# The shift's rounded part straight from ScalarE, its full value and difference on GpSimd, in an attention kernel on one core

## The chip, the cores and the metric

The program runs on one core of a Trainium2 chip. The metric is the device time of one execution in microseconds. A core has five engines with queues of their own: TensorE (PE, with its weight loads shown apart as PEld), VectorE (DVE), ScalarE (ACT), GpSimd (POOL) and SyncE (SP), which here issues nearly all DMAs. Each works through its queue in the order in which the program was built, and waits at an instruction until what that needs is ready.

## The reference

One block of a transformer with adaptive layer norm, on 2048 rows of 512, with 32 heads of 16:

```python
def _A_ref(x, wqkv, wo):
    ...
    scores = jnp.einsum("bhqd,bhkd->bhqk", q, k) * (Dh ** -0.5)
    p = _softmax(scores, axis=-1)
    o = jnp.einsum("bhqk,bhkd->bhqd", p, v)
    return (lambda x, *d: x.transpose(*d))(o, 0, 2, 1, 3).reshape(B, S, D) @ wo
...
mod = (_silu(c) @ w_mod).reshape(c.shape[0], 6, 1, -1)
sa, ca, ga, sb, cb, gb = (mod[:, 0], mod[:, 1], mod[:, 2], mod[:, 3], mod[:, 4], mod[:, 5])
h = _layernorm(x, axis=-1) * (1 + ca) + sa
x = x + ga * _A_ref(h, A_wqkv, A_wo)
h = _layernorm(x, axis=-1) * (1 + cb) + sb
x = x + gb * _B_ref(h, B_w1, B_w2, B_w3, B_w4)
```

`_B_ref` is a mixer: layer norm, `w1` and gelu, shifts along the rows, `w2`, then layer norm, `w3` and gelu, `w4`, with residuals. The change is inside the softmax of `_A_ref`.

## The kernel before

**Precision.** Matrices are used as a rounded upper part (type `F32R`) and the difference to it, so a product takes three matmuls (`mm3`, lines 359, 361 and 363 of its lines in the profile, for `k`, `q`, `v` and the mixer's `w`).

**Units.** Attention goes through 64 units: four chunks of 512 queries, and in each 16 pairs of heads. A unit has 16 steps, one for each 128 keys, and each step has two halves, one for each head `j` of the pair. A step does the following.

- *Maxima.* `max_part` (lines 996 and 992) works 24 steps ahead: PE computes scores with queries on the partitions into a bank `mb`, VectorE takes their row maximum into `mx`. One reduction of 128x512 for each half step.
- *Shift.* When the last maximum of a unit is there, `max_fin` (lines 1042 to 1045) makes the unit's shift, 26 ln 2 minus the maximum, for each of the 8 x 128 queries: VectorE's small reduction `mf`, the full value in place on ScalarE, its rounded upper part `nm[:, 0]` on ScalarE, the difference `nm[:, 1]` on GpSimd. Eight small DMAs (`shift_rows`) write both parts as two more rows of the queries' tile `qtl`, whose partners in the keys' tile `kst` are rows of ones: the matmul itself adds the shift.
- *Scores and exponentials.* `score_part` (lines 1012 and 1008): PE computes the shifted scores with keys on the partitions into a bank `sc`, ScalarE writes their exponential as 32-bit whole numbers into `pt`.
- *Halving.* `p_low` (line 1061 on GpSimd, or line 156 on ScalarE) turns the low 16 bits of 128x1024 of these into half-precision numbers. The planner picks the engine that it thinks is free first.
- *Output.* `pv_part`: PE multiplies the upper words (line 1086) and, two blocks later, the halved low words (line 1083) by `v` into one bank `pv`. At a unit's end ScalarE copies it to `ac` (line 1103), PE transposes it (`ot`, line 1113), and ScalarE (line 1120), VectorE and GpSimd (line 1124) divide by the sums into `osb`.

Seven banks are shared by `mb`, `sc` and the other work's results. Each is free again when VectorE or ScalarE has read it.

**What sets the order.** The program is written by a planner, `Sched`: it keeps a supposed time for each engine (`T`) and puts instructions into the queues as those times advance. A chain like the one of the shift is a list of (engine, supposed ns, function); `misc` puts its parts between the exponentials (ACT), maxima (DVE) and halvings (POOL) where they fit. The supposed costs so decide where everything else goes, and which engine gets a halving:

```python
g, a = [max(sch.T[e], ready) for e in "GA"]
if g > a + LACT:
```

**Stages.** The layer norm, the modulation and the first projections come first. Units 0 to 12 have the rest of the projections `v`, `k` and `q` between their steps, as the planner's fill (with ScalarE's `qk` roundings, line 353, and weight pieces, lines 881 to 896). Units 13 to 61 are attention alone. After that come the output projection and the mixer (`tail`), which begin within units 62 and 63.

Of the kernel before, what the change touches and what calls it, by code (L numbers as in the profile page):

```python
# [14 lines left out]
AF = mybir.ActivationFunctionType  # L15
OP = mybir.AluOpType
# [16 lines left out]
PEXP = PBITS * 0.6931471805599453  # L33
# [297 lines left out]
def kernel(ctx, tc, A_x, A_wqkv, A_wo, B_w1, B_w2, B_w3, B_w4, c, w_mod, out):  # L331
    nc = tc.nc
    te, act, dve, pool, dma = nc.tensor, nc.scalar, nc.vector, nc.gpsimd, nc.sync
# [21 lines left out]
    def mark(key):  # L355
        return None, 0, lambda: done.add(key)
# [623 lines left out]
    def max_part(m, j):  # L980

        u, i = divmod(m, 16)
        c, g = divmod(i, 4)
        if u not in mxs:
            mxs[u] = at.tile([P, 2, 4, NC], F32, name="mx", tag="mx", bufs=2)
        x, b = bank("mb")
        ready, sm.t[x] = sm.t[x], LATE
        r = slice(64 * j, 64 * j + 62)
        lhs = qst[u][r, (g // 2) * 256:(g // 2 + 1) * 256].rearrange("p (n l) -> p l n", l=2)[:, g % 2]

        def after(e):
            end = sch.crit("D", 605, e + PX, lambda: dve.reduce_max(mxs[u][:, j, g, c:c + 1], b, axis=AX.X))  # L992
            sm.t[x] = end + XP["D"]
            if (c, g, j) == (NC - 1, 3, 0):
                max_fin(u)
        return ready, lambda: te.matmul(b, lhs, kst[u % 3][r, c * CH:(c + 1) * CH], start=True, stop=True), after  # L996
# [32 lines left out]
    def max_fin(u):  # L1029
        mf = at.tile([P, 8], F32, name="mf", tag="mf", bufs=2)  # L1030
        nm = at.tile([P, 2, 8], F32R, name="nm", tag="nm", bufs=2)
        mx = mxs.pop(u)

        def shift_rows():
            for j in range(2):
                for i in range(2):
                    r = 64 * j + 62 + i
                    for h in range(2):
                        sch.dma(dma.dma_start,
                                qst[u][r:r + 1, h * 256:(h + 1) * 256].bitcast(F32).rearrange("o (p l) -> o p l", l=2),  # L1040
                                nm[:, i, 4 * j + 2 * h:4 * j + 2 * h + 2].bitcast(F32))
        sch.chain(("D", 85, lambda: dve.reduce_max(mf.rearrange("p (j g) -> p j g", j=2), mx, axis=AX.X)),
                  ("A", 100, lambda: act.activation(mf, mf, AF.Copy, scale=-1.0, bias=PEXP)),
                  ("A", 100, lambda: act.activation(nm[:, 0], mf, AF.Copy)),
                  ("G", 250, lambda: pool.tensor_tensor(nm[:, 1], mf, nm[:, 0], op=OP.subtract)),
                  (None, 0, shift_rows), mark(("shift", u)), prio=0, ready=sch.T["D"])

    def p_low(s):
# [553 lines left out]
    for k, blk in enumerate(blocks + [[]] * (LAG + CPER)):  # L1602
# [35 lines left out]
        low = sorted(e_exp)  # L1638
# [92 lines left out]
```

## Time and profile before

| | |
|---|---|
| runs | 2022.35, 2021.24, 2019.19 us; median 2021.24 |
| profiled execution | 2021.44 us, of which the span from first to last instruction is 2019.7 us |
| granted TensorE clock over the span | 0.992 |
| shifts | 64, one for each unit, first at 121 us, last at 1492 us |
| line 1043 / 1044 (ScalarE) | 64 each, median 220 / 209 ns |
| line 1045 (GpSimd) | 64, median 203 ns |
| shift DMAs `qtl<-nm` | 512, 1.0 KB each, median 2.0 us to landing |
| halvings | 953 on GpSimd, mean 1367 ns; 71 on ScalarE |

In rows of groups stand line, engine, operation, what is written and read, shapes and count, then busy us and mean ns of one, then the engine's idle time just before them and what ended it. In rows of a stretch stand its ends, its length, busy time (and count) of PE, PEld, DVE, ACT and POOL, then the granted clock, the DMA engines' busy share and GB/s. In rows of the chain, the work that ended last followed backwards, stand start, length and name. In rows of the timeline a run of equal instructions is one row, with its start, its length from first start to last end, and the count behind the x.

### The profile page before, as it was taken

The numbers are of one execution on the slowest core, as the hardware profiler recorded it, in microseconds if no ns is written. First come the engines' busy times: TensorE is split into PE (matmuls) and PEld (weight loads), VectorE is DVE, ScalarE is ACT, GpSimd is POOL, SyncE is SP. The second block draws the span as 40 slices with busy tenths as digits, with TensorE's granted clock in tenths as the row PEclk, the third lists the DMA queues.
The fourth block names the chain that finished last, engine by engine and source line by source line (L and its number), as shares of the span: only waits on it lengthen the run. The fifth ranks groups of instructions, "written<-read, shape, count | busy, mean of one in ns | idle before, by whom it ended". The sixth has DMA issues, their size and how long they took to land.

```text
span 2019.7 us, 41655 instructions
## 1 busy us (share of the span) xinstructions
PE 1934.4 (96%) x14456; PEld 1162.1 (58%) x14456; DVE 1656.3 (82%) x2979; ACT 1510.2 (75%) x3085; POOL 1571.9 (78%) x1488
## 2 busy tenths in 40 slices
PE   7999999999999999999999999999998999999999
PEld 5755545454444444444444444444455878898998
DVE  6398888879999999999999999999975886556443
ACT  6438987768999999999999999999985544344443
POOL 6349988879999999999999999999996554435222
PEclk9989999999999999999999999999999999999999
DMA  8777675445343434444443435354414676553541
GB/s 295 233 204 192 151 187 155 135 130 124 86 92 87 91 88 83 96 82 97 81 98 75 104 72 107 72 136 126 99 46 158 230 261 265 226 200 116 201 153 68
DMA packets 185508, 278.01 MB, mean 138 GB/s; under 512 B 117104, under 2 KB 127856, under 8 KB 169008
## 3 DMA queue, kind: packets, MB, share of 16 engines
q1 hardware_dynamic: 181792, 267.20, 49.1%
q10 hardware_dynamic: 2304, 4.20, 0.6%
q0 software_dynamic: 1200, 3.93, 0.5%
q8 instruction: 115, 1.88, 0.4%
q14 instruction: 97, 0.79, 0.1%
HBM read 211.81 MB, written 62.91 MB: 136 GB/s over the span
## 4 chain that ended last, share of the span: by engine, by line
PE 61%; DVE 16%; ACT 9%; issue 6%; POOL 4%; DMA 3%; SPq 0%; ACTq 0%; POOLq 0%; DVEq 0%
PE mb L996 13%; DVE mx L992 12%; PE pv L1086 9%; PE sc L1012 8%; ACT pt L1008 7%; PE w L363 5%; PE w L359 5%; PE w L361 5%; PE pv L1083 4%; PE ot L1113 3%; POOL pt L1061 2%; PE xT L1247 1%; POOL trs L1356 1%; PE v L359 1%; DMA wr<-Ws 1%
## 5 line engine op out<-in xcount | busy, mean ns | idle before, releaser
L1061 POOL TENSOR_SCALAR pt<-pt 128x1024 f16<-128x1024 uint16 x953 | 1248.3, 1367 | 79.9 <-ACT pt L1008 76.7
L992 DVE TENSOR_REDUCE mx<-mb 128x1 f32<-128x512 f32 x2048 | 1250.0, 681 | 72.7 <-PE mb L996 63.5
L1008 ACT ACTIVATE pt<-sc 128x512 int32<-128x512 f32 x2048 | 1060.9, 614 | 123.5 <-PE mb L996 97.1
L996 PE MATMUL mb<-kst,qtl 62*128 62x512 f32 x2048 | 781.1, 461 | 20.5 <-ACT pt L1008 10.0
L1012 PE MATMUL sc<-qtl,kst 64*128 64x512 f32 x2048 | 739.3, 449 | 4.6 <-DVE mx L992 1.8
L996 PEld LDWEIGHTS mb<-kst,qtl 62*128 62x128 f32 x2048 | 358.9, 193 | 233.7 <-ACT pt L1008 160.4
L1012 PEld LDWEIGHTS sc<-qtl,kst 64*128 64x128 f32 x2048 | 336.6, 185 | 185.4 <-DVE mx L992 118.7
L1086 PE MATMUL pv<-pt,vst 128*32 128x512 f16 x4096 | 384.8, 397 | 20.6 <-ACT ac L1103 20.6
L1460 POOL TENSOR_TENSOR g<-sq,g 128x256 fp32r<-128x256 f32 (+1 forms) x124 | 96.8, 785 | 188.9 <-ACT g L1459 176.6
L1083 PE MATMUL pv<-pt,vst 128*32 128x512 f16 (+1 forms) x2048 | 220.8, 389 | 2.5 <-POOL pt L1061 2.4
L1086 PEld LDWEIGHTS <-vst 128*32 128x32 bf16 x4096 | 91.8, 93 | 227.2 <-issue 208.8
L361 PE MATMUL w<-A,wr 128*128 128x256 f32 (+1 forms) x520 | 153.4, 295 | 0.3 <-DVE A L349 0.3
L359 PE MATMUL w<-A,wr 128*128 128x256 f32 (+1 forms) x520 | 153.2, 295 | 0.3 <-ACT A L353 0.3
L363 PE MATMUL w<-A,wr 128*128 128x256 f32 (+1 forms) x520 | 153.1, 294 | 0.0
L1456 ACT ACTIVATE sq<-w 128x256 f32<-128x256 f32 (+1 forms) x130 | 52.1, 401 | 127.0 <-PE w L363 117.5
L363 PE MATMUL w<-wr,g 128*128 128x512 f32 x270 | 106.5, 394 | 3.1 <-POOL g L1460 3.1
L359 PE MATMUL w<-wr,g 128*128 128x512 f32 x270 | 106.9, 396 | 1.8 <-DMA wr<-Ws 1.8
L361 PE MATMUL w<-wr,g 128*128 128x512 f32 x270 | 106.1, 393 | 0.0
L1438 DVE SCALAR_TENSOR_TENSOR sq<-sq,w 128x256 f32<-128x256 f32 (+1 forms) x130 | 58.1, 449 | 56.5 <-ACT sq L1458 56.3
L359 PEld LDWEIGHTS w<-A,wr 128*128 128x128 f32 x520 | 98.7, 190 | 1.7 <-ACT A L353 0.5
L361 PEld LDWEIGHTS w<-A,wr 128*128 128x128 f32 x520 | 98.7, 190 | 1.6 <-DVE A L349 0.5
L363 PEld LDWEIGHTS w<-A,wr 128*128 128x128 f32 x520 | 98.6, 190 | 0.5 <-issue 0.5
(156 smaller groups left out, 2131.6 us busy)
## 6 DMA issues: line engine op xcount, KB each, us to landing
wr<-Ws SPq DMA_DIRECT2D x66, 1024.0 KB, 5.2
vst<-Vs SPq DMA_DIRECT2D x64, 768.0 KB, 5.7
kst<-Ks SPq DMA_DIRECT2D x126, 384.0 KB, 6.1
Ws<-wr SPq DMA_DIRECT2D x14, 1024.0 KB, 5.0
qtl<-Qs SPq DMA_DIRECT2D x128, 96.0 KB, 4.3
Vs<-vt SPq DMA_DIRECT2D x32, 384.0 KB, 4.2
Ks<-qk SPq DMA_DIRECT2D x16, 512.0 KB, 3.8
Qs<-qk SPq DMA_DIRECT2D x16, 512.0 KB, 3.0
```

The source lines that it names most:

```text
L359: te.matmul(o, lh, rh, start=first, stop=False)
L361: te.matmul(o, lh, rl, start=False, stop=False)
L363: te.matmul(o, ll, rh, start=False, stop=last)
L992: end = sch.crit("D", 605, e + PX, lambda: dve.reduce_max(mxs[u][:, j, g, c:c + 1], b, axis=AX.X))
L996: return ready, lambda: te.matmul(b, lhs, kst[u % 3][r, c * CH:(c + 1) * CH], start=True, stop=True), after
L1008: ea = sch.crit("A", 480, e + PX, lambda: act.activation(pt[s][:, j], b, AF.Exp))
L1012: return ready, lambda: te.matmul(b, kst[u % 3][r, kt * P:(kt + 1) * P], qst[u][r], start=True, stop=True), after
L1061: e_low[s] = XP["G"] + sch.crit("G", 1345, ready, lambda: pool.tensor_scalar(o, i, 0.5, 1.0, op0=OP.mult, op1=OP.mult))
L1083: te.matmul(acc[r:r + n, :], v[:, kt + i, c:c + n].bitcast(F16), pt[s + i].bitcast(F16)[:, j, 0::2], start=False, stop=kt == NKT - 2, skip ...
L1086: te.matmul(acc[r:r + 32, :], v[:, kt, r:r + 32], pt[s].bitcast(F16)[:, j, 1::2], start=kt == 0, stop=False, skip_group_check=True)
L1113: te.matmul(b[:, t * n:(t + 1) * n], ac[:, t * P:(t + 1) * P], smat.rearrange("p j d -> p (j d)"), start=True, stop=True)
L1460: ("G", cG(n), lambda: pool.tensor_tensor(lo, sq, hi, op=OP.subtract)), (None, 0, end), bank=b)
```

## The change

ScalarE no longer makes the full value. It computes the shift from the maxima and rounds it in one instruction (new line 1047). GpSimd makes the full value in place from the maxima and then the difference (new lines 1035 and 1036). The planner's list has one ScalarE entry of 100 ns fewer, and GpSimd's is 450 in place of 250.

```diff
@@ max_fin
         mx = mxs.pop(u)
 
+        def low():
+            pool.tensor_scalar(mf, mf, -1.0, PEXP, op0=OP.mult, op1=OP.add)
+            pool.tensor_tensor(nm[:, 1], mf, nm[:, 0], op=OP.subtract)
+
         def shift_rows():
...
         sch.chain(("D", 85, lambda: dve.reduce_max(mf.rearrange("p (j g) -> p j g", j=2), mx, axis=AX.X)),
-                  ("A", 100, lambda: act.activation(mf, mf, AF.Copy, scale=-1.0, bias=PEXP)),
-                  ("A", 100, lambda: act.activation(nm[:, 0], mf, AF.Copy)),
-                  ("G", 250, lambda: pool.tensor_tensor(nm[:, 1], mf, nm[:, 0], op=OP.subtract)),
+                  ("A", 100, lambda: act.activation(nm[:, 0], mf, AF.Copy, scale=-1.0, bias=PEXP)),
+                  ("G", 450, low),
                   (None, 0, shift_rows), mark(("shift", u)), prio=0, ready=sch.T["D"])
```

The order of the queues changes with it. Lines from 1034 on have numbers that are 3 or 4 higher: 1047 stands for 1043 and 1044, 1035 and 1036 for 1045, 1064 for 1061, 1106 for 1103, 1123 for 1120 and 1127 for 1124; line 156 keeps its number.

First, GpSimd around the shifts of units 27 and 28, in attention alone (`pt` are halvings, `osb` is a finished unit's division). Before:

```order
L1045 TENSOR_TENSOR nm<-mf,nm 128x8
L1061 TENSOR_SCALAR pt<-pt 128x1024 x15
L1045 TENSOR_TENSOR nm<-mf,nm 128x8
L1124 TENSOR_TENSOR osb_7627<-sm,rc 128x4x32
L1061 TENSOR_SCALAR pt<-pt 128x1024 x11
```

Now:

```order
L1036 TENSOR_TENSOR nm<-mf,nm 128x8
L1064 TENSOR_SCALAR pt<-pt 128x1024 x15
L1035 TENSOR_SCALAR mf<-mf 128x8
L1036 TENSOR_TENSOR nm<-mf,nm 128x8
L1127 TENSOR_TENSOR osb_7627<-sm,rc 128x4x32
L1064 TENSOR_SCALAR pt<-pt 128x1024 x11
```

One instruction more stands at the same place; the halvings around it are unmoved.

Second, ScalarE in units 30 and 31, from the copy `ac` in the one to that in the other (`pt<-sc` are exponentials, `pt<-pt` on line 156 is a halving). Before:

```order
L1008 ACTIVATE pt<-sc 128x512 x15
L1103 ACTIVATE ac<-pv 128x512
L1008 ACTIVATE pt<-sc 128x512 x3
L1120 ACTIVATE sm<-ot 128x136
L1008 ACTIVATE pt<-sc 128x512 x6
L156 ACTIVATE pt<-pt 128x1024
L1008 ACTIVATE pt<-sc 128x512 x3
L1043 ACTIVATE mf<-mf 128x8
L1044 ACTIVATE nm<-mf 128x8
L1008 ACTIVATE pt<-sc 128x512 x21
L156 ACTIVATE pt<-pt 128x1024
L1103 ACTIVATE ac<-pv 128x512
```

Now:

```order
L156 ACTIVATE pt<-pt 128x1024
L1008 ACTIVATE pt<-sc 128x512 x3
L1106 ACTIVATE ac<-pv 128x512
L1008 ACTIVATE pt<-sc 128x512 x3
L1123 ACTIVATE sm<-ot 128x136
L1008 ACTIVATE pt<-sc 128x512 x12
L1047 ACTIVATE nm<-mf 128x8
L1008 ACTIVATE pt<-sc 128x512 x6
L156 ACTIVATE pt<-pt 128x1024
L1008 ACTIVATE pt<-sc 128x512 x12
L1106 ACTIVATE ac<-pv 128x512
```

The halving that stood right ahead of unit 31's copy has gone from there, and one has come three exponentials ahead of unit 30's. The same happens in units 42 and 43 and in 54 and 55; in unit 13 the halving ahead of the copy goes too. In the other units between 16 and 61 ScalarE's row is unmoved but for the missing line 1043, or moved by a few places.

Third, ScalarE in units 11 and 12, from one shift to the next, where the last projections are (`qk<-q` is the rounding behind 12 fill matmuls of `q`). Before:

```order
L1044 ACTIVATE nm<-mf 128x8
L1008 ACTIVATE pt<-sc 128x512 x12
L353 ACTIVATE qk_163<-q 128x512
L1008 ACTIVATE pt<-sc 128x512 x9
L1103 ACTIVATE ac<-pv 128x512
L1008 ACTIVATE pt<-sc 128x512 x6
L353 ACTIVATE qk_165<-q 128x512
L1120 ACTIVATE sm<-ot 128x136
L1008 ACTIVATE pt<-sc 128x512 x9
L1043 ACTIVATE mf<-mf 128x8
```

Now:

```order
L1047 ACTIVATE nm<-mf 128x8
L1008 ACTIVATE pt<-sc 128x512 x12
L353 ACTIVATE qk_165<-q 128x512
L1008 ACTIVATE pt<-sc 128x512 x9
L1106 ACTIVATE ac<-pv 128x512
L1008 ACTIVATE pt<-sc 128x512 x3
L1123 ACTIVATE sm<-ot 128x136
L1008 ACTIVATE pt<-sc 128x512 x12
L1047 ACTIVATE nm<-mf 128x8
```

The last rounding of `q` now stands one unit's copy earlier: the projections end in unit 11.

## The prediction

> **What bounds the kernel now.** I read the first part of the page, then a table of the stages by stretch, then groups, waits and chain of the long middle stretch, and last one of its units instruction by instruction.
>
> ```profile
> span 2019.7 us, 41655 instructions
> PE 1934.4 (96%) x14456; PEld 1162.1 (58%) x14456; DVE 1656.3 (82%) x2979; ACT 1510.2 (75%) x3085; POOL 1571.9 (78%) x1488
> ```
>
> PE is the fullest engine, but its busy time counts overlapping, modelled matmuls; the shares also average over stages. The stretches show more (length, then busy time of PE, weight loads, VectorE, ScalarE, GpSimd):
>
> ```profile
> 0.00:131.10 131.10, 116.61 (x544) 82.33 (x544) 80.41 (x167) 59.57 (x118) 54.53 (x73) 0.97 0.78 240
> 131.10:477.10 346.00, 335.88 (x2553) 180.63 (x2554) 287.59 (x490) 271.81 (x563) 303.04 (x259) 0.98 0.63 164
> 477.10:1468.50 991.40, 959.17 (x8168) 454.76 (x8170) 950.47 (x1654) 916.69 (x1814) 951.04 (x811) 1.00 0.44 94
> 1468.50:1535.00 66.50, 63.69 (x490) 33.55 (x490) 42.28 (x78) 50.83 (x104) 61.11 (x61) 1.00 0.20 61
> 1535.00:2019.70 484.70, 459.08 (x2712) 410.86 (x2710) 295.55 (x594) 211.32 (x488) 202.18 (x287) 0.99 0.52 191
> ```
>
> Units 0 to 12 fill the second row, with projections mixed in; the third is attention alone, half of the span, where PE, VectorE and GpSimd are all busy 96 to 97% and ScalarE 92%. The change puts work on and off two engines of a balanced loop. From 550.9 to 1468.5 us, 45 units, the groups (count, busy us, mean ns, idle before) and waits (total, times, longest) are:
>
> ```profile
> L992 DVE TENSOR_REDUCE mx<-mb 128x1 f32<-128x512 f32 x1441 | 876.0, 681 | 31.1 <-PE mb L996 24.9 <-PE sc L1012 3.1
> L1061 POOL TENSOR_SCALAR pt<-pt 128x1024 f16<-128x1024 uint16 x661 | 860.5, 1363 | 31.9 <-ACT pt L1008 29.4
> L156 ACT ACTIVATE pt<-pt 128x1024 f16<-128x1024 uint16 x60 | 82.5, 1375 | 0.0
> L1043 ACT ACTIVATE mf<-mf 128x8 f32<-128x8 f32 x45 | 10.7, 237 | 0.0
> L1044 ACT ACTIVATE nm<-mf 128x8 fp32r<-128x8 f32 x45 | 9.4, 209 | 1.6 <-ACT mf L1043 0.2
> L1045 POOL TENSOR_TENSOR nm<-mf,nm 128x8 fp32r<-128x8 f32 x45 | 9.1, 203 | 2.4 <-ACT nm L1044 2.0
> ```
> ```profile
> PEld mb L996 <- ACT pt L1008: 132.8, 390, 0.8
> PE pv L1086 <- ACT ac L1103: 17.5, 15, 1.2
> ```
>
> VectorE idles 31 us in 918, so its maxima are the floor. PE waits most for ScalarE's exponentials to free banks. One stall is regular: 15 times in 45 units PE stands 1.17 us until ScalarE has copied the finished output (`ac`).
>
> The chain of that stretch gives the removed instruction a share:
>
> ```profile
> by line: PE mb L996 20.9%; DVE mx L992 18.8%; PE pv L1086 14.4%; PE sc L1012 12.6%; ACT pt L1008 12.5%; issue 7.6%; PE pv L1083 5.5%; PE ot L1113 4.5%; ACT ac L1103 1.0%; POOL pt L1061 0.6%; ACT mf L1043 0.4%; ACT pt L156 0.4%; DVE mf L1042
> ```
>
> 0.4% of 917.6 us is 3.7 us; at 0.25 us a time that is 15 of 45 units. One such place, out of the chain's pieces (start, us, what):
>
> ```profile
> 774.77 1.30 ACT pt L1008 x3
> ...
> 776.22 0.25 ACT mf L1043
> ...
> 776.49 0.02 ACT nm L1044
> ...
> 776.60 0.02 ACT pt L1008
> ...
> 778.21 0.50 PE mb L996
> ...
> 788.50 0.08 ACT pt L156
> 788.58 1.00 issue
> 789.58 0.60 ACT ac L1103
> ```
>
> PE's matmul at 778.21 waits for an exponential that stood behind the two small instructions. Twelve us later the same unit shows the `ac` stall: line 156, the 1.375 us halving of low words that the planner sometimes gives to ScalarE, stands right ahead of the copy.
>
> **The change part by part.** *ScalarE loses line 1043.* The exponentials end at 776.07 and the next starts at 776.60, 0.53 us. With the rounding alone, its lead-in (776.07 to 776.22) and its offset to the next exponential (776.49 to 776.60) remain, 0.26. The gain is 0.27 us where it is on the path: 15 × 0.27 = 4.05 us. In the other 30 units ScalarE's delay ends in VectorE's unbroken row of maxima and the gain is nothing; that cover is the floor itself. The Trainium skill prices this lower: "ScalarE: Activation LUTs", section "What ACT_TABLE_LOAD costs", gives 186 ns plus 0.833 ns an element, with 93 ns overlap back to back, so an estimate of 0.10 us for eight elements and 1.5 us in place of 4.05; with all of that kept the sum below would be −0.1 and the time 2021.3 us. The trace does not agree here, since the second instruction reads the first's result and cannot overlap it.
>
> *GpSimd gains an instruction, in a pair where the second reads the first.* Such pairs stand at the program's start (start, us):
>
> ```profile
> 1.41 0.22 POOL L392 TENSOR_TENSOR smat<-ident 128x17 f32<-128x17 f32 x1 [0.34 <-DVE mone L398]
> 1.71 0.22 POOL L393 TENSOR_TENSOR smat<-smat,ident 128x17 f32<-128x17 f32 x1
> ```
>
> From start to start 0.30 us, which I take for each of 64 shifts. The first of the pair overwrites `mf`, which ScalarE reads, so it cannot run beside ScalarE. Queued behind the pair are the halvings (line 1061), and PE's low matmuls (line 1083) wait for those. In the unit above:
>
> ```profile
> 778.10 0.20 POOL L1045 TENSOR_TENSOR nm<-mf,nm 128x8 fp32r<-128x8 f32 x1
> 778.26 3.95 POOL L1061 TENSOR_SCALAR pt<-pt 128x1024 f16<-128x1024 uint16 x3
> ```
> ```profile
> 782.56 0.40 PE L1083 MATMUL pv<-pt,vst 128*32 128x512 f16 x4
> ```
>
> The third halving ends at 782.21 and is used at 782.56: 0.35 us of room. PE 0.27 earlier and GpSimd 0.30 later overdraw it by 0.22, which leaves 0.05 of the gain; if GpSimd's string starts 0.27 earlier too, nothing is overdrawn and 0.27 stays. The string begins behind work that PE and VectorE release, so I lean to the second: 0.20 kept, 15 × 0.20 = **−3.0 us**, ends −0.75 and −4.05. Where GpSimd waits for ScalarE before the pair, the shorter ScalarE part pays for it.
>
> *The shift's eight DMAs* stay in place on SP in the middle stretch. The first two need only ScalarE's part and start 0.27 earlier; those of the difference start up to 0.30 later only where GpSimd is behind. Cost nothing, covered as the one row of PE's waits for them shows; without the cover it would be 0.30 for each shift.
>
> ```profile
> DMA qtl<-nm: 0.2, 1
> ```
>
> *The planner's costs moved.* Of 1024 halvings, 77 instead of 71 go to ScalarE. PE's order of scores, maxima and outputs in units 13 to 61 is the same but for the place of one small step in three units, and the tail behind the last unit is the same on the four compute engines. In four places of the middle (units 13, 31, 43, 55) line 156 no longer stands ahead of the `ac` copy: 1.17 us less each. In exchange one stands three exponentials ahead of an earlier copy; it costs 1.375 less the idle time that ScalarE has between exponentials, as here:
>
> ```profile
> 780.03 3.05 ACT L1008 ACTIVATE pt<-sc 128x512 int32<-128x512 f32 x6 [0.41 <-PE mb L996]
> ```
>
> So 0.97 lost, 1.17 won: 4 × −0.20 = **−0.8 us**, ends −4.7 (nothing lost) and +3.9 (nothing won).
>
> *The projections move.* Ten of its q matmuls leave unit 12, unit 6 has 10 in place of 29 fill matmuls, unit 5 has 42 for 31. Units 11, 12 and 13 hold 30, 10 and none:
>
> ```profile
> 428.50:455.90 27.40, 26.86 (x206) 14.01 (x202) 22.35 (x38) 20.11 (x40) 21.44 (x18) 1.00 0.46 141
> 455.90:477.10 21.20, 21.20 (x178) 10.72 (x176) 18.92 (x34) 17.09 (x35) 18.76 (x17) 1.00 0.56 153
> 477.10:498.00 20.90, 19.43 (x170) 9.56 (x170) 19.61 (x35) 18.94 (x38) 19.90 (x18) 1.00 0.40 87
> ```
>
> Ten cost unit 12 only 0.3 us; in a full unit each costs (27.4 − 20.9) / 30 = 0.22. Moved, they cost 2.2 − 0.3 = **+1.9 us**, ends 0 (other gaps hide them) and +3.8 (twice, for longer runs). GpSimd's extra 13 × 0.30 there is met by three halvings fewer. From 1468.5 to 1535 us GpSimd is the fullest but PE and one pair stands there: **+0.3 us**.
>
> Sum: −3.0 − 0.8 + 1.9 + 0.3 = −1.6 us on the profiled execution's 2021.4 us (span 2019.7 and 1.7 around it; the median of the runs is 2021.2): **2019.8 us**.
>
> **The rivals.** *All of it lands (faster).* ScalarE's 4.05 us stay and the four copies are never late elsewhere: −4.05 − 4.7 + 1.9 + 0.3 = −6.6, so 2014.9 us. For it speaks the chain, against it the 0.35 us of room. 30%.
>
> *GpSimd becomes the bound (slower).* In the middle it idles 31.9 us before halvings, 0.7 a unit. If in two of three units its string has no gap to take the pair, PE's low matmuls come 0.30 later there: 30 × 0.30 = 9.0, no ScalarE gain, −0.8 + 1.9 + 0.3: 2031.8 us. It decides from the point where a low matmul's room of 0.35 us is spent in units other than the fifteen. Against it speaks that 29.4 of those 31.9 us are waits for exponentials: it is mostly ahead of its input. 13%. The Trainium skill leans this way: "GPSIMD Engine Reference", section "Engine selection", keeps elementwise work off this engine; the pair's 0.30 us against 0.27 saved agrees with it.
>
> *The new order is worse (slower).* Both ends of the planner's terms: −3.0 + 3.9 + 3.8 + 0.3 = +5.0, so 2026.4 us. For it: nothing in the rows says that the new places of line 156 are better. 17%.
>
> **How the numbers follow.** 0.2% is 4.0 us, about what a measurement of this kernel can tell from no change, as the runs' 2019.2 to 2022.4 suggest. The forecast (2016 to 2024 by itself) has 40%: 9 of these below 2017.2, 31 within. With the first rival faster is 0.39; the third gives 2 to same, so 0.33; slower is 0.13 + 0.15 = 0.28. The range 2012 to 2028 holds all but the second rival and some tails.
>
> **What would show it.** Right: line 1047 at 0.21 us with no second instruction; PE's wait before the maxima behind it shorter by up to 0.27; GpSimd's pair 0.30 from start to start; 12 stalls of 1.17 us before `ac` in those 45 units instead of 15; unit 12 near 20.9 us and the units before it longer. Wrong: PE waiting for line 1064 in most units, PE waiting for the shift's DMAs, a middle stretch longer than 991 us, or units 0 to 12 changed by over 4 us.

## The result, and the profile after

| | before | after |
|---|---|---|
| median of the runs | 2019.84 us (2018.7 to 2022.4) | 2032.56 us (2027.1 to 2033.6) |
| ratio | | 1.0055, 95% interval 1.0040 to 1.0069 |
| profiled execution | 2021.44 us, span 2019.7 | 2027.06 us, span 2025.3 |

The change made the kernel slower, by 0.55% in the ratio and 12.7 us between the medians, where 2019.8 us was predicted with a range of 2012 to 2028. The profiled execution is the quickest of its runs and only 5.6 us above the one of before; a second one, below (e1), spans 2033.2 us.

The page's head and the stretches of after, at the bounds used for before (ends, length, busy time and count of PE, PEld, DVE, ACT, POOL, then granted clock, DMA share, GB/s):

```profile
span 2025.3 us, 41277 instructions
PE 1949.2 (96%) x14456; PEld 1170.0 (58%) x14456; DVE 1657.1 (82%) x2979; ACT 1504.8 (74%) x3027; POOL 1578.9 (78%) x1546
131.10:477.10 346.00, 335.93 (x2592) 180.51 (x2592) 291.39 (x497) 277.00 (x563) 308.85 (x274) 0.99 0.63 166
477.10:1468.50 991.40, 966.14 (x8096) 457.06 (x8096) 943.94 (x1639) 904.39 (x1755) 949.18 (x848) 1.00 0.44 93
```

The same bounds cut other work now: more of it fits into the second row (PE x2592 for x2553), less into the long one (VectorE x1639 for x1654). So I compared by unit instead: the start of a unit's first score matmul (line 1012), after minus before.

| stretch | change, us | what is in it |
|---|---|---|
| start to unit 3 | −1.4 | |
| units 3 to 15 | −4.1 | a clock drop that the execution before had and this one has not: 3.4 |
| units 16 to 28 | −0.5 | a clock drop before: 0.6 |
| units 29 to 55 | +4.8 | units 30, 32, 42, 44, 54 each +1.15 to +1.45; units 31, 43, 55 each −1.0; a clock drop 0.75 |
| unit 56 | +4.0 | 24.75 us for 20.72 |
| units 57 to 62 | 0.0 | |
| unit 63 to the end | +2.9 | one clock drop more: 3.4; e6, e11 and e14 below, which have neither the new order nor the pair of GpSimd instructions, lose as much to the clock there, so this is not the change |

The shift's instructions and PE's waits in the same 45 units (groups, then waits: total, times, longest):

```profile
L1047 ACT ACTIVATE nm<-mf 128x8 fp32r<-128x8 f32 x45 | 10.4, 232 | 0.0
L1036 POOL TENSOR_TENSOR nm<-mf,nm 128x8 fp32r<-128x8 f32 x45 | 9.1, 202 | 4.1 <-POOL mf L1035 0.7
L1035 POOL TENSOR_SCALAR mf<-mf 128x8 f32<-128x8 f32 x45 | 8.9, 197 | 6.6 <-ACT nm L1047 3.3
```
```profile
PE pv L1089 <- ACT ac L1106: 15.5, 15, 1.2
PE sc L1012 <- DMA qtl<-nm: 3.3, 3, 2.0
PE sc L1012 <- DVE mx L992: 1.5, 3, 0.7
```

The instructions cost about what was expected. New are the last two rows: the score matmul waits. What the second of them hides shows in the shift of unit 30, one of those where a halving (line 156) now stands three exponentials ahead of the rounding. The timeline of after, engine by engine:

```profile
810.09 1.40 ACT L156 ACTIVATE pt<-pt 128x1024 f16<-128x1024 uint16 x1
811.31 1.59 ACT L1008 ACTIVATE pt<-sc 128x512 int32<-128x512 f32 x3
812.73 0.26 ACT L1047 ACTIVATE nm<-mf 128x8 fp32r<-128x8 f32 x1
...
813.02 5.98 SPq L135 DMA_DIRECT2D qtl<-nm  x8
...
814.80 0.20 POOL L1035 TENSOR_SCALAR mf<-mf 128x8 f32<-128x8 f32 x1
815.08 0.20 POOL L1036 TENSOR_TENSOR nm<-mf,nm 128x8 fp32r<-128x8 f32 x1
...
820.59 0.51 PE L1012 MATMUL sc<-qtl,kst 64*128 64x512 f32 x2 [0.66 <-DVE mx L992]
```

The maxima were ready at 810.74, the rounding ends 2.25 us behind them; GpSimd is behind by three halvings and makes the difference 2.3 us later still. SyncE, whose third DMA waits for the difference, issues the eight from 813.02 to 819.00; a row lands 2.0 us from its issue, the last at 820.4, and the second score matmul, which needs it, starts at 820.59. The row names VectorE, which had long been done: it was the DMA. Before, in the same unit, the rounding ended 1.28 us behind the maxima, the difference 0.6 us later, and the last row landed 1 us ahead of its matmul:

```profile
817.82 0.21 ACT L1044 ACTIVATE nm<-mf 128x8 fp32r<-128x8 f32 x1
...
818.43 0.21 POOL L1045 TENSOR_TENSOR nm<-mf,nm 128x8 fp32r<-128x8 f32 x1
...
818.05 4.99 SPq L135 DMA_DIRECT2D qtl<-nm  x8
```

In unit 56 something else meets: the mixer's first loads. ScalarE's four loads of input rows, 8 us into unit 56 before, now stand at its start together with a 1 MB weight load, ahead of the next keys. Timelines of before and of after (ACTq is ScalarE's issue of a DMA, SPq SyncE's), then the clock of after (last three columns: clock, DMA share, GB/s):

```profile
1362.35 0.39 ACTq L1281 DMA_DIRECT2D x<-in_A_x_dram  x1
...
1362.77 1.41 ACTq L1281 DMA_DIRECT2D x<-in_A_x_dram  x3
```
```profile
1352.85 0.44 ACTq L1284 DMA_DIRECT2D x<-in_A_x_dram  x1
1353.33 0.93 ACTq L1284 DMA_DIRECT2D x<-in_A_x_dram  x2
...
1352.98 0.59 SPq L135 DMA_DIRECT2D wr<-Ws  x1
...
1356.04 0.47 PE L1012 MATMUL sc<-qtl,kst 64*128 64x512 f32 x1 [1.99 <-DMA qtl<-nm]
```
```profile
1353.10:1356.10 3.00, 1.01 (x6) 0.42 (x3) 2.47 (x5) 1.48 (x3) 3.00 (x4) 1.00 0.93 263
1356.10:1359.10 3.00, 3.00 (x23) 1.26 (x23) 0.94 (x2) 1.51 (x3) 2.39 (x2) 0.67 1.03 403
```

PE waits 2.0 us for the last shift row, and then its clock falls.

### The profile page after: what moved, and what is told of

The parts are those of the page before. It is cut to its first block, busy times and chain, and to the rows that moved or that the text cites. A ratio compares the mean times of both kernels' runs of the same rounds, so it can differ in the third digit from the quotient of the medians.

```text
span 2025.3 us, 41277 instructions
## 1 busy us (share of the span) xinstructions
PE 1949.2 (96%) x14456; PEld 1170.0 (58%) x14456; DVE 1657.1 (82%) x2979; ACT 1504.8 (74%) x3027; POOL 1578.9 (78%) x1546
## 4 chain that ended last, share of the span: by engine, by line
PE 67%; DVE 12%; ACT 7%; issue 5%; POOL 4%; DMA 4%; SPq 0%; ACTq 0%; POOLq 0%; DVEq 0%
PE mb L996 15%; PE pv L1089 11%; PE sc L1012 10%; DVE mx L992 9%; PE w L363 5%; PE w L359 5%; PE w L361 5%; PE pv L1086 5%; ACT pt L1008 5%; PE ot L1116 3%; POOL pt L1064 2%; DMA wr<-Ws 1%; PE xT L1250 1%; POOL trs L1359 1%; PE v L359 1%
## 5 line engine op out<-in xcount | busy, mean ns | idle before, releaser
L1012 PE MATMUL sc<-qtl,kst 64*128 64x512 f32 x2048 | 730.8, 447 | 8.5 <-DVE mx L992 3.7
L1086 PE MATMUL pv<-pt,vst 128*32 128x512 f16 (+1 forms) x2048 | 233.3, 389 | 3.9 <-POOL pt L1064 3.7
L156 ACT ACTIVATE pt<-pt 128x1024 f16<-128x1024 uint16 x77 | 106.9, 1388 | 0.0
L1086 PEld LDWEIGHTS <-vst 128*32 128x32 f16 (+1 forms) x2048 | 64.9, 94 | 66.2 <-issue 42.0
L359 PEld LDWEIGHTS w<-A,wr 128*128 128x128 f32 x520 | 100.1, 192 | 1.7 <-ACT A L353 0.5
```

The source lines that it names most:

```text
L156: fn()
L359: te.matmul(o, lh, rh, start=first, stop=False)
L1012: return ready, lambda: te.matmul(b, kst[u % 3][r, kt * P:(kt + 1) * P], qst[u][r], start=True, stop=True), after
L1086: te.matmul(acc[r:r + n, :], v[:, kt + i, c:c + n].bitcast(F16), pt[s + i].bitcast(F16)[:, j, 0::2], start=False, stop=kt == NKT - 2, skip ...
```

## The experiments

The theories: the *order theory*, that the moved instructions cost all of it (late rows, the loads at unit 56) and the exchange of instructions nothing; and the *instruction theory*, that GpSimd's pair and what waits for it do. In "old order" kernels the planner is given the old list, so that every other instruction stands as before. The edits are shown shortened: words stand for code that is left out, and `one` is the new rounding instruction.

**e1, the changed kernel again.**

> The changed kernel once more, for a second profile. Both theories expect a ratio to before near 1.0055 (2027 to 2034 us). Order theory: units 0 to 12 again 5 to 6 us shorter than before, units 30, 42 and 54 again with a wait of 0.6 us for the shift's rows ahead of the second score matmul, 1.2 to 1.4 us lost at each of the units with a halving ahead of the rounding, and what is lost behind unit 55 in the same places if it is the order, elsewhere if it is chance.

Measured: 2032.97 us, 1.0061 (1.0049 to 1.0074). Units 29 to 55 lose 5.0 us (0.75 a clock drop) and unit 56 7.0: this time PE waited 3.4 us for the next keys (waits, then clock):

```profile
PE mb L996 <- DMA kst<-Ks: 3.4, 1, 3.4
```
```profile
1369.90:1372.90 3.00, 3.00 (x18) 2.62 (x14) 0.67 (x3) 0.49 (x2) 0.00 (x0) 0.50 0.04 10
```

The places are the order's. The stretch behind unit 63 lost 5.9 us against before; the clock accounts for it (11.9 us lost to it there, 3.4 before).

**e2, new instructions, old order**

```diff
-  ("A", 100, one), ("G", 450, low),
+  ("A", 100, lambda: None), ("A", 100, one), ("G", 250, low),
```

> The new instructions at the places of the old order. Order theory: 0.999 to 1.001, no unit changed by more than 0.3 us, since the difference comes 0.67 us later only in every third unit, where 0.9 us of room stand ahead of the second score matmul. Instruction theory (GpSimd's pair, and rows that land later): slower by 0.3 to 0.6%, 2026 to 2033 us, with waits for the shift's rows in most units.

Measured: 2021.97 us, 1.0007 (0.9994 to 1.0020), no unit from 16 to 62 changed by more than 0.3 us but where a clock drop stood before, as the order theory expected.

**e3, old instructions, new order**

```diff
+  def full(): the two ScalarE instructions
-  ("A", 100, one), ("G", 450, low),
+  ("A", 100, full), ("G", 450, the old difference),
```

> The old instructions at the places of the new order. Order theory: slower by 0.3 to 0.6% (2026 to 2032 us), units 0 to 12 some 5 us shorter, and the loss at units 30 to 33, 42 to 45, 54 to 57. Instruction theory: 0.997 to 0.998 (2014 to 2016 us), the 5 us of units 0 to 12 kept and nothing lost behind them.

Measured: 2026.24 us, 1.0030 (1.0018 to 1.0042); units 29 to 55 +3.0 us (4.0 and 4.3 in after and e1 without their clock drops), unit 56 +4.7. The order costs some 6 us by itself, the instructions in the old order nothing that can be told; together they cost about 12, so they meet somewhere. One place is units 30, 42 and 54: in e3 the rounding is 0.2 us later still, but the last row lands 0.4 us earlier, since the difference follows sooner, and no wait for rows shows there; in units 32 and 44 PE waits in both. These three units are 2.2 us shorter than in after, but others give some back, and units 29 to 55 together differ by 1.0 to 1.3 us; the rest of the 6 is in unit 56 and behind unit 63, where the profiles scatter as much, and stays open. The order theory holds for half, with the pair as a part of the other.

**e4, rounded rows first**

```diff
-            for j in range(2):
-                for i in range(2):
+            for i in range(2):
+                for j in range(2):
```

> The changed kernel with the four DMAs of the rounded part issued first and the four of the difference behind them, so that only four stand behind the wait for GpSimd. If the rows that land late are what costs: the last row lands 0.7 to 1.0 us earlier wherever GpSimd is behind, the waits of 0.6 us at units 30, 42 and 54 and 0.4 at 32 and 44 go, and the time is 2 to 5 us below the changed kernel's. If the halving ahead of the rounding costs by delaying exponentials and maxima: the waits for rows go, but PE waits as long for exponentials, and the time is that of the changed kernel within 1 us.

Measured: 2026.59 us, 1.0031 (1.0021 to 1.0042), 6 us below e1 in the same comparison, more than expected. Units 29 to 55 lose 1.7 us (e1 5.0); the waits are gone in units 30, 42 and 54, but 0.2 and 0.6 us remain in 32 and 44.

**e7, the seven halvings behind the rounding**

```diff
+  held = []   # seven of ScalarE's halvings: kept back, issued right behind nm
```

> The changed kernel with seven halvings (units 14, 30, 32, 42, 44, 54, 56) moved on ScalarE from one to four places ahead of the rounding to right behind it, and all else where it was. If they cost by making the shift's rows late: the rounding ends 0.9 to 1.3 us earlier there, the waits of 0.4 to 0.65 us for rows go, each of the three groups (units 30 to 33, 42 to 45, 54 to 55) loses 0.3 us or less instead of 1.3 to 1.7, and unit 56 is as long as before or only waits for keys; 3 to 5 us below the changed kernel. If they cost by holding up exponentials: the waits for rows go, but the groups lose as much.

Measured: 2030.66 us, 1.0052 (1.0039 to 1.0065). The stretch of units 29 to 33, for before, after, e4, e7, and e10 (both edits, and the loads moved):

```profile
804.69:905.67 100.98, 98.43 (x842) 46.56 (x840) 97.31 (x170) 93.31 (x186) 97.84 (x85) 1.00 0.44 90
```
```profile
798.64:901.24 102.60, 100.84 (x843) 47.36 (x841) 97.80 (x171) 93.50 (x182) 97.48 (x88) 1.00 0.42 88
```
```profile
799.71:901.12 101.41, 100.64 (x842) 47.50 (x840) 97.65 (x170) 93.36 (x182) 97.33 (x88) 1.00 0.43 89
```
```profile
798.56:900.54 101.98, 100.76 (x842) 47.42 (x840) 97.81 (x171) 93.47 (x182) 97.41 (x88) 1.00 0.44 88
```
```profile
798.77:899.81 101.04, 100.43 (x842) 47.57 (x841) 97.69 (x171) 93.22 (x182) 97.46 (x88) 1.00 0.43 89
```

Lost against before: 1.6, then 0.4, 1.0 and 0.06. Late rows are the cause, but not as e7 expected: its rounding ends 1.2 us sooner in unit 30, yet the difference does not, since GpSimd's queue sets it, and PE still waits 0.56 us. With the four rounded rows issued first, SyncE uses the time in which it waited for GpSimd: all eight go out in 4.98 us instead of 5.98 (e4, unit 30):

```profile
814.05 4.98 SPq L135 DMA_DIRECT2D qtl<-nm  x8
```

e7's own miss: the wait stayed in units 30, 42 and 54 and went only in 32 and 44. Only both edits cure all five.

**e5, e8: the row loads 8 us later, alone and with the edits of e4 and e7**

```diff
+        yield sch.wait(8000.0)
         for t in range(TPC):
             x1t[t] = ...
             act.dma_start(x1t[t], x_d[...])
```

> The changed kernel with the mixer's four loads of the input's rows (256 KB each, issued by ScalarE) issued 8 us later, behind unit 57's keys instead of ahead of them. Collision theory: unit 56 takes 20.7 to 21.3 us instead of 24.7 to 27.8, no wait of 2 to 3.4 us for keys or shift rows and no half clock behind it, 4 to 7 us less than the changed kernel (2025 to 2029). If the weight load of 1 MB ahead of the keys is enough for the wait, or the wait is chance: no change.

> The changed kernel with the three edits together: rounded rows first, the seven halvings behind the rounding, the mixer's row loads later. If late rows and the collision are the whole loss: nothing lost behind unit 14, so the gain of units 0 to 14 (4 to 6 us in the profiles) stays: 2015 to 2018, 0.1 to 0.3% below before. If the gain of the early units is chance (a clock that happened not to drop): 2019 to 2021.

Measured: 2029.12 us, 1.0048 (1.0035 to 1.0061), and 2024.48, 1.0021 (1.0012 to 1.0030). The units before 56 behave as hoped in e8 (+0.1 us from unit 29 to 55), but unit 56 still takes 26.7 and 26.0 us. No wait above 0.2 us for a DMA's data is left there; ScalarE's queue stood (timeline of e5):

```profile
1361.11 4.93 ACTq L1286 DMA_DIRECT2D x<-in_A_x_dram  x1
1366.08 1.41 ACTq L1286 DMA_DIRECT2D x<-in_A_x_dram  x3
1367.53 0.28 ACT L1124 ACTIVATE sm<-ot 128x136 f32<-128x136 f32 x1 [4.39 <-issue]
...
1368.36 0.69 PE L997 MATMUL mb<-kst,qtl 62*128 62x512 f32 x1 [3.87 <-ACT pt L1009]
```

A single issue took 4.93 us (4.57 in e8); the exponentials stood behind it, and PE behind them. Both expectations missed this. Why it took so long is not shown: in the kernel before, the first of the four took 0.39 us with more loads under way (384 KB of keys, 1 MB of weights and 768 KB of values; here keys and values).

**e6, the row loads moved up in the kernel before, nothing else**

```diff
         for i in range(BR):
             rings["0"].add([("wr", BR)])
+            if i == 1: the four loads
             yield sch.wait(T0W)
```

> The kernel before with only those four loads moved up, from 8 us into unit 56 to the end of unit 55, behind the second weight load. Collision theory: unit 56 takes 24 to 28 us instead of 20.7, with a wait of 2 us or more for keys or shift rows and a clock of 0.5 to 0.9 in the 6 us behind it, 2023 to 2027. If only the new order's late shift rows make them harmful: no change from before (2019 to 2022).

Measured: 2025.30 us, 1.0025 (1.0012 to 1.0037). The loss comes at the end of unit 55 (+5.2 us) with 0.8 more in unit 56: the four issues take 0.33 to 0.39 us each, but the last starts 4.2 us behind the end of the third, just when an earlier shift row's DMA, whose semaphore it uses, has landed (5.3 us from its issue, not 2.0, among the loads); the exponentials stand behind it and PE waits 3.9 us. So the loads' place alone is worth some 5 us, without any of the change. I had expected a wait for keys; it was ScalarE's queue.

**e9, e10, e15: the loads in the middle of unit 56, the last two with the edits of e4 and e7, the last issued by SyncE**

```diff
-        for t in range(TPC): ... act.dma_start(...)
+        later.append(the four loads)     # issued behind the exponentials of step 10 of unit 56
-                act.dma_start(...)       # e15 alone
+                dma.dma_start(...)
```

> The changed kernel with the four loads of the input's rows issued 12 to 13 us into unit 56, when the keys and values of unit 57 have landed, and no other instruction moved. If what costs there is the loads' meeting with unit 57's keys and ScalarE standing at their issue: unit 56 in 20.7 to 21.5 us, no half clock between 1340 and 1400, the loads issued in 0.4 to 0.5 us each, 4 to 7 us less than the changed kernel (2025 to 2028). If the 1 MB of weights at the end of unit 55 is enough: a wait of 1.5 us or more remains and the time is that of the changed kernel.

> The changed kernel with rounded rows first, the seven halvings behind the rounding and the row loads 12 to 13 us into unit 56. The variant units then cost 0.5 to 1 us in all instead of 4, unit 56 nothing: 2017 to 2020.5, within 0.2% of before. If the new order has a further loss: 2023 or more.

> The changed kernel with rounded rows first, the seven halvings behind the rounding, and the four row loads in the middle of unit 56 issued by SyncE instead of ScalarE. If ScalarE standing 2.3 us at their issue is what was left there: unit 56 takes 20.7 to 20.9 us, no wait above 0.6 us and no half clock behind it, 2 to 3 us less than with ScalarE's issue. If the loads themselves (1 MB of traffic) delay the next rows: unit 56 stays at 22 us or more.

Measured: 2027.74 us, 1.0046 (1.0033 to 1.0059); 2021.93, 1.0011 (1.0003 to 1.0020); 2023.54, 1.0013 (1.0003 to 1.0023). Units 55 and 56 together, for before, after, e9, e10, e15:

```profile
1333.12:1375.15 42.03, 40.68 (x342) 18.93 (x338) 40.01 (x71) 38.96 (x77) 39.63 (x35) 1.00 0.68 186
```
```profile
1332.87:1377.89 45.02, 42.64 (x342) 20.00 (x341) 40.35 (x71) 38.97 (x76) 39.67 (x36) 0.96 0.65 175
```
```profile
1333.56:1379.37 45.81, 43.45 (x342) 19.79 (x340) 40.19 (x70) 38.80 (x76) 39.96 (x37) 0.93 0.64 170
```
```profile
1328.45:1371.99 43.54, 41.91 (x342) 19.76 (x341) 40.11 (x70) 38.71 (x76) 40.04 (x37) 0.96 0.67 179
```
```profile
1331.52:1372.89 41.37, 41.24 (x343) 19.45 (x342) 40.19 (x71) 38.76 (x76) 39.57 (x36) 1.00 0.71 190
```

e10 with ScalarE's issue, e15 with SyncE's: 43.54 and 41.37 us, at clocks of 0.96 and 1.00. In e10 the four issues, unhindered, still held ScalarE for 2.3 us:

```profile
1363.09 0.39 ACTq L1299 DMA_DIRECT2D x<-in_A_x_dram  x1
1363.52 1.86 ACTq L1299 DMA_DIRECT2D x<-in_A_x_dram  x3
...
1366.13 0.51 PE L997 MATMUL mb<-kst,qtl 62*128 62x512 f32 x1 [1.60 <-ACT pt L1011]
```

So ScalarE's standing cost PE 1.6 us there. The pair of runs alone would not show it, since the time of the loads moved too: SyncE's queue did not wait for the exponentials and issued them 5.6 us into the unit, ScalarE 14.4 us in e10. What e15 does show is that the 1 MB itself can pass without a loss, and the kernel before shows that the standing can: there the four issues held ScalarE for 1.8 us 8 us into the unit, which took 20.72 us, as units 38 and 50 did (20.73 and 20.72).

e10's time lies between its two expectations. e15's median is no better than e10's, though its profiled span lost next to nothing there (0.3 us in unit 56): the runs scatter by more than these 2 us. e9 is a miss: unit 56 takes 25.6 us, though the time is within the expected: its loads came 17 us in, ScalarE stood for them, and the keys were still 0.7 us late behind the weights.

**e11, ScalarE's part alone; e12, GpSimd's part alone; both in the old order**

```diff
e11
-  ("A", 100, line 1043), ("A", 100, line 1044), ("G", 250, lambda: pool.tensor_tensor(nm[:, 1], mf, nm[:, 0], ...))
+  ("A", 100, lambda: None), ("A", 100, one), ("G", 250, lambda: pool.tensor_tensor(nm[:, 1], nm[:, 0], nm[:, 0], ...))
e12
+  pool.tensor_scalar(mf, mf, 1.0, 0.0, op0=OP.mult, op1=OP.add)   # ahead of the difference
```

> The old order with ScalarE's line 1043 gone and nothing added on GpSimd: its one instruction stays, but writes zero as the difference, so the full value is left out. If the prediction's term was right that ScalarE's 0.27 us are on the path in 15 of 45 units and GpSimd's pair took them back: three units (such as 33 to 36) take 60.7 instead of 61.0 us, 2015 to 2017 us in all. If the floor set by the maxima and the banks takes them: 61.0 us for three units, 2019 to 2021.

> The kernel before in its order with one more 128x8 instruction on GpSimd ahead of the difference (it multiplies the full value by one). If GpSimd had no room: 0.36 us more in two of three units or so, 2030 us. If its place is covered: the difference lands 0.36 us later and takes that from the 0.9 us of room ahead of the second score matmul; three units stay at 61.0 us, 2019 to 2022, with 1 to 2 us for the units that had only 0.1 to 0.2 us of room.

**e13, a third GpSimd instruction in e2; e14, no GpSimd instruction and no rows for the difference**

```diff
e13  (in low, between the two)
+  pool.tensor_scalar(mf, mf, 1.0, 0.0, op0=OP.mult, op1=OP.add)
e14  (to e11)
-  ("G", 250, the difference), and its four DMAs
+  ("G", 250, lambda: None)
```

> The new instructions at the places of the old order with a third 128x8 instruction on GpSimd between the two (the full value times one). If GpSimd's string is what takes ScalarE's 0.3 us per three units back, its room is now spent: three units (33 to 36 and the like) take 61.25 to 61.4 us, against 61.0 with two instructions and 60.7 with one, and the time is 4 to 6 us above that with two (2025 to 2028). If the gain is lost for another reason (rows that land late, the waits of the pair): 61.0 us for three units still, 2021 to 2024.

> The old order with the rounded part as the whole shift: ScalarE's one instruction, no GpSimd instruction and no DMAs for the difference (its rows in the queries' tile stay zero; the full value and the difference are left out, which the softmax divides out, since every key of a query has the same shift). If the ScalarE part alone makes the gain: 2012 to 2015 us, 60.7 us for three units, as with GpSimd's single instruction. If GpSimd's and SyncE's strings still hold something: 60.4 to 60.6 us and 2008 to 2012.

Measured: e11 2013.30 us, 0.9970 (0.9959 to 0.9982); e12 2022.60, 1.0019 (1.0007 to 1.0031); e13 2033.51, 1.0065 (1.0049 to 1.0081); e14 2014.00, 0.9966 (0.9953 to 0.9978). Three ordinary units (33 to 35), for before, e12, e2, e13, e11, e14:

```profile
886.31:947.32 61.01, 59.08 (x508) 27.93 (x504) 58.66 (x103) 56.59 (x113) 58.67 (x51) 1.00 0.43 90
```
```profile
881.45:942.45 61.00, 59.07 (x509) 28.02 (x505) 58.70 (x103) 56.60 (x113) 59.06 (x54) 1.00 0.42 89
```
```profile
883.48:944.44 60.96, 59.32 (x508) 28.27 (x504) 58.73 (x103) 56.09 (x110) 59.19 (x54) 1.00 0.44 89
```
```profile
888.52:950.26 61.74, 59.51 (x509) 28.23 (x505) 58.89 (x103) 56.25 (x110) 59.81 (x57) 1.00 0.41 88
```
```profile
879.99:940.60 60.61, 58.96 (x509) 28.16 (x505) 58.68 (x103) 56.03 (x110) 58.62 (x51) 1.00 0.43 90
```
```profile
878.96:939.58 60.62, 58.97 (x508) 28.05 (x504) 58.66 (x103) 56.07 (x110) 58.30 (x48) 1.00 0.42 90
```

The counts in the last bracket give GpSimd's instructions: 51 are one a unit, 54 two, 57 three, 48 none. With ScalarE's gain, 60.6 us with none or one, 61.0 with two, 61.7 with three; without it, 61.0 with one or two. That is a room that is spent. Around the shift of unit 28 in e2 and in e11 (timelines):

```profile
775.15 0.50 PE L996 MATMUL mb<-kst,qtl 62*128 62x512 f32 x1 [0.21 <-ACT pt L1008]
...
779.49 0.79 PE L1087 MATMUL pv<-pt,vst 128*32 128x512 f16 x4
```
```profile
772.49 0.51 PE L996 MATMUL mb<-kst,qtl 62*128 62x512 f32 x1 [0.23 <-ACT pt L1008]
...
776.84 0.40 PE L1083 MATMUL pv<-pt,vst 128*32 128x512 f16 x4
```

Both shorten the wait for the exponential from 0.46 to 0.21 and 0.23, as predicted. But the low matmuls take 0.79 us in e2, held between their halves, and 0.40 in e11: the third halving ends 6.63 us behind the maxima in e2, 6.24 in e11 and 6.23 before. GpSimd's string is 0.40 us later, PE 0.25 earlier, the room was 0.35. e13's waits name it (total, times, longest):

```profile
PE pv L1088 <- POOL pt L1066: 7.0, 23, 0.5
```

e13 lost more than its expected 2025 to 2028 us: the third instruction makes the string 0.36 us longer and three units 0.8 us, of which these waits are a part; where the others lie is open.

e12's median is 0.2% above before with no unit changed; its profiled execution lost 13.6 us to the clock behind unit 63, before 3.4. Whether the pair does that, as in e1, or chance, stays open.

**A version that beats both** is e11 or e14, which do not differ measurably: 0.30 and 0.34% below before. They leave out the difference, so the shift is the rounded maximum alone, the same for all keys of a query, and the division by the sums takes it out.

## Why the prediction was wrong, point by point

- *What bounds the kernel*: no run contradicts it. The stalls before `ac` moved as foretold: 12 of 1.17 us and three of 0.5 now (15.5 us in 15), for 15 of 1.17.
- *ScalarE loses line 1043*: right in place and size. 4.05 us were worked out; alone it is 0.4 us in three units and 4.9 in the 45 (912.7 us from unit 17 to 62 in e11, 917.6 before), and PE's wait shrank by 0.25. The lower price (the Trainium skill, "ScalarE: Activation LUTs", "What ACT_TABLE_LOAD costs"; an estimate of 1.5 us) does not agree with that.
- *GpSimd gains an instruction*: **a failed step**. Both readings stood there, "overdraw it by 0.22", and 0.20 kept if the string started earlier too. I leaned to the second; the first is what happens. The string in front of the pair is one unbroken row of halvings (5.36 us for four in the quoted unit) and starts no earlier. The second instruction makes the string 0.40 us later, not 0.30, so nothing of the −3.0 was kept: e2 equals before.
- *The shift's eight DMAs, "cost nothing"*: **a failed step**. The cover, one wait of 0.2 us before, was read where GpSimd had time, and its own price without the cover (0.30) used only the instruction's length. Where a halving has come ahead of the rounding (units 30, 32, 42, 44, 54) the last row lands 0.6 to 2.0 us later behind the maxima than before, and PE waits 0.4 to 0.66 us.
- *The planner's costs moved, −0.8*: **the failed step that cost most with the next**. I priced the halvings at the copies. The 1.17 won is there, as 1.0 in units 31, 43 and 55; the 0.97 lost is 1.15 to 1.45 in five units, since two more halvings of a group went ahead of roundings, which the term did not look at. Measured +4.0 us (units 29 to 55 without the drop), the upper end of the term, but by another mechanism, so the end is luck. With the rows in time (e10) units 30 to 32, 42 to 44 and 54 to 55 change by −0.2, +0.2 and −0.5 us, about the −0.2 that was foretold for each.
- *The loads of the mixer*: not in the sum at all. The prediction says that the tail behind the last unit keeps its order, which is so; its first loads are issued within units 55 and 56, on SyncE's and ScalarE's queues, and ScalarE's moved by 8.7 us. Unit 56 lost 4 to 7 us.
- *The projections, +1.9*: not seen. Units 3 to 15 are 4.1 us shorter in after, but the profiled execution before had a clock drop there that cost 3.4. In runs without one they are 2.9 to 4.6 us shorter in the new order (seven kernels) and 2.5 to 4.9 in the old (e6, e11 to e14): the move is worth about nothing. Unit 12 takes 19.2 us, less than the 20.9 foretold.
- *The rivals*: "the new order is worse" had the right sign and not the mechanism; "GpSimd becomes the bound" had the right place but, by itself, cancels the gain (e2) instead of losing 9 us; it takes a third instruction (e13) to lose about that.

## What to carry to other kernels

When a planner moves work, walk along every queue at the moved places, DMA issues too, and ask of each instruction that came to stand behind something new what its result feeds: here a rounding that feeds eight DMAs. A gain on one engine counts only up to the room of the next one in the same unit, and if the mover's partner gets longer, subtract before leaning to the kinder reading. And before work is moved to another engine, see whether it is needed: the difference was not.

## What the runs showed of the hardware

**The clock falls for short waits.** In the run before, PE waited 1.44 us and then ran 6.8 us (303.5 to 310.3) at a clock of 0.50:

```profile
302.07 0.49 PE L1012 MATMUL sc<-qtl,kst 64*128 64x512 f32 x1 [1.44 <-ACT pt L1008]
```

After's 1.40 us wait at the same place (306.1) brought no drop. The time lost to the clock in a stretch, summed over 10 us slices, comes in steps of 1.7 us: 1.7, 3.4, 5.1, 6.8, 8.5, 10.2. That is half a clock for 3.4 us, or several times that. The Trainium skill, "TensorE: Matmul & The Clock Gate", section "What's actually happening", has a half clock after an idle window of about 3.4 us that runs freely; the halves and the 3.4 us agree with the rows, but waits of 1.4 to 2.0 us were followed by a drop here at times, and no run shows what decides. By these figures a wait of 2 us can cost up to 5.4 (an estimate, 2.0 and 3.4; unit 56 of e3, with a wait of 1.9, lost 4.7). It is a part of the scatter between executions: of 29 of the kernel before, the longest (span 2026.1 us) had a mean clock of 0.987, and the seven shortest (2014.4 to 2015.5) had 0.991 to 0.995.

**An engine stands while it issues a DMA.** ScalarE needed 0.33 to 0.62 us for most loads of 256 KB, with little under way (e10) or with three larger loads (before), but 4.93 and 4.57 us for one in e5 and e8, with its exponentials behind it; no run shows what decides. In e6 it stood 4.2 us ahead of an issue, until another DMA had landed. The Trainium skill, "DMA: Bandwidth & Descriptors", section "Issuing engines are not separate DMA queues", calls the sequencer's time for an issue usually small beside the DMA; 0.39 us of 8.2 to landing in the kernel before agree with that, 4.93 of 7.4 in e5 do not. What the standing costs depends on what stands behind it: PE waited 1.6 us in e10, and unit 56 lost nothing before.
